# One block pair of a retention and softplus feed-forward kernel moved from plain products to the seven-product scheme

## The chip, the cores and the metric

The kernel runs on one core of a Trainium2 chip. The metric is the device time of one execution in microseconds (us), the median over repeated runs. Engines are named as in the profile: PE is TensorE, PEld its weight loads, DVE is VectorE, ACT is ScalarE, POOL is GpSimd, SP is SyncE, whose queue issues nearly all DMAs (SPq).

## The reference

Eight sequences of 576 positions, eight heads of 64, go through a retention: scores with a decay that depends on the distance, masked to earlier positions, times the values. The 4608 x 512 result is multiplied by w_in (512 x 2048), passed through a softplus and multiplied by w_out (2048 x 512).

```python
ret = scores * Dmat[None, :, :, :]        # scores = q k^T / 8, Dmat = gamma_h ** (i - j) for i >= j, else 0
attn = np.matmul(ret, v)
x = attn.transpose(0, 2, 1, 3).reshape(B * S, H * D)
h = x @ w_in
g = np.maximum(h, 0.0) + np.log1p(np.exp(-np.abs(h)))
return (g @ w_out).astype(np.float32)
```

## The kernel before, in words

All matrix products of the feed-forward part are float32-accurate products of split numbers: every operand is kept as a head and a rest, and one product of a 256 x 128 block of weights with 512 tokens is six matmuls of 128 x 128 x 512 (three terms, two row tiles; `product`, L1094). Tokens are dealt in units of 512, NUNIT = 9 of them. The attention part runs in chunks of 128 tokens: a *group* (`chunk_products`) does the scores and state sums of one chunk and the values of the chunk before it, in some hundred small matmuls, and is put between the large products of the feed-forward part. It writes the PSUM banks `two` and `third`, and for some chunks also `acc`. After the group DVE empties these banks (`scores_out`, `halves_out`, `states_out`), and SP loads the keys and the values of the next group (`next_steps`: `load_keys`, `load_rest`); POOL scales the values (`scale_values`, L229) before the next group's matmuls may read them. For most groups PE also waits, before the second half of its state sums, for a one-column ACT copy (`marker`, L419).

Unit 0 is done in the opening. Units 1 and 2 are the *first pass*, the part that changes. Their hidden layer is cut into NJ = 8 pairs of column blocks. A pair can be done in two ways:

- *Plain*: two slots (`plain_slot`) in unit 1 and two in unit 2. A slot has two products into one bank (`product(bank, xa, True)`, `product(bank, xb)`), ACT's softplus, the head and rest of the result, the outputs of the slot before (`output_some(CPU)`, 12 matmuls, L597 with L605 for unit 0) and, in some slots, a group.
- *Seven-product* (`strassen_pair`): seven products cover both units at once. The products need combined inputs (blocks T1, T2, T3, NT4, made by `start_combined` from four 128 x 256 operations and `finish_combined` from one ACT copy and one DVE subtraction for each of four columns of 128 tokens) and combined weights (`prepare`: load a pair, `prepare_whole`, `prepare_sums`, `prepare_split`, `prepare_store`). The results of unit 2 are kept in DRAM (`kept_dram`) and fetched after unit 2's plain slots, in the *kept loop* (`kept_parts`).

With PLAIN = 4 the order is: 8 slots of unit 1 (pairs 0 to 3), four seven-product pairs (4 to 7), 8 slots of unit 2, the kept loop. Then come three passes that use seven products throughout (`full_pair`, `full_phase`), which the change doesn't touch but which need all combined weights (`sums_dram`), the split second weights (`wout_dram`, written by `raw_store`) and their combined form (`outs_dram`, by `whole_out`, `combine_out`, `split_out`, `store_out`).

The order of each engine's instructions is the order in the program, written out by hand: `schedule(...)` lists which helper runs in which slot, and `jobs`, `blocks`, `starts` and `before` are its places in a slot. Weight blocks come through a ring of 7 tiles: each `product` takes one and issues the load of the block seven products on (`block_load`, L759). The SP queue runs in order, so a DMA that waits holds up those behind it.

In the seven-product pair the bank `acc` takes four products in turn, and is read between them:

```python
product(acc, T3)
nc.vector.tensor_add(c[1], acc, c[1])
...
output_some(2 if few else -(-len(outputs) // 2))
product(acc, NT4)
```

`few` is true when only one slot's four outputs are pending, which is so in the first such pair alone.

## Time and profile before

| what | value |
| --- | --- |
| median of 3 runs | 811.35 us (810.53 to 812.31) |
| profiled execution | 811.05 us, span 809.1 us |
| PE busy | 802.9 us, 99% of the span |
| DVE, ACT, POOL busy | 573.5, 395.7, 135.9 us |
| granted TensorE clock | 1.00 throughout |

The span is what the profile's rows cover; the profiled execution's own time is 1.95 us longer than its span. All times of rows are us from the start of the span. In the rows, a line such as "acc<-xt,ring" names the tile written and the tiles read.

### The profile page before, as it was taken

The page shows a single profiled execution, that of the slowest core. Times are in us where ns is not written, and L with a number is a line of the kernel's source. Part 1 is how long each engine was busy: PE and PEld are TensorE (multiplying, and loading weights), DVE is VectorE, ACT ScalarE, POOL GpSimd, SP SyncE. Part 2 cuts the span into 40 slices and gives each one's busy share as a digit, 9 for nine tenths or more (in the row PEclk, how much of TensorE's full clock was granted, in tenths as well). Part 3 has the DMA queues.
Part 4 walks back from the last instruction along what each step waited for, and adds up shares of the span by engine and source line. Part 5 has one row for each costly group of instructions (what it writes and reads, how often), then busy time and mean ns, then how long its engine had stood idle before and what let it go on. Part 6 is the DMA issues. An engine that isn't in the chain of part 4 may idle for free.

```text
span 809.1 us, 18743 instructions
## 1 busy us (share of the span) xinstructions
PE 802.9 (99%) x7363; PEld 660.7 (82%) x7363; DVE 573.5 (71%) x946; ACT 395.7 (49%) x691; POOL 135.9 (17%) x211
## 2 busy tenths in 40 slices
PE   8999999999999999999999999999999999999998
PEld 6788888888888888888888888888888888888886
DVE  6988878866657973888579974546679944335785
ACT  6877773344333443454345654343355734435553
POOL 4331333611113420121121001111100000000000
PEclk9999999999999999999999999999999999999999
DMA  9999698898987984799987778778767776666665
GB/s 357 366 310 383 233 355 292 303 347 270 311 300 258 383 317 169 255 325 332 298 268 235 216 242 252 240 245 257 214 182 219 220 245 192 193 194 194 205 209 172
DMA packets 150488, 213.59 MB, mean 264 GB/s; under 512 B 10881, under 2 KB 114817, under 8 KB 150401
## 3 DMA queue, kind: packets, MB, share of 16 engines
q1 hardware_dynamic: 150304, 212.40, 78.8%
q8 instruction: 59, 0.97, 0.5%
q14 instruction: 29, 0.23, 0.1%
q10 hardware_dynamic: 96, 0.00, 0.0%
HBM read 169.36 MB, written 42.99 MB: 262 GB/s over the span
## 4 chain that ended last, share of the span: by engine, by line
PE 97%; DMA 2%; ACT 0%; DVE 0%; issue 0%; SPq 0%; DVEq 0%
PE acc L1094 22%; PE sum L1399 21%; PE third L1094 11%; PE y L597 11%; PE h L558 6%; PE y L605 5%; PE two L1094 5%; PE two L1399 4%; PE third L1399 2%; PE acc L1399 2%; PE third L253 2%; PE two L236 2%; PE two L325 1%; PE two L337 1%; DMA raw<-whole 1%; DMA part<-first 0%
## 5 line engine op out<-in xcount | busy, mean ns | idle before, releaser
L1094 PE MATMUL acc<-xt,ring 128*128 128x512 f32 x780 | 196.6, 389 | 0.0
L1399 PE MATMUL sum<-parts,ring 128*128 128x512 f32 (+1 forms) x723 | 173.8, 391 | 0.0
L1094 PEld LDWEIGHTS acc<-xt,ring 128*128 128x128 f32 x780 | 146.3, 188 | 30.6
L1399 PEld LDWEIGHTS sum<-parts,ring 128*128 128x128 f32 x723 | 134.2, 188 | 28.3
L1393 DVE TENSOR_TENSOR parts<-g,parts 128x512 fp32r<-128x512 f32 x168 | 113.5, 692 | 45.8 <-ACT parts L1389 44.6
L1389 ACT CAST parts<-g 128x512 fp32r<-128x512 f32 x168 | 103.7, 622 | 68.0 <-PE sum L1399 24.8
L1094 PE MATMUL third<-xt,ring 128*128 128x512 f32 x408 | 102.8, 389 | 0.0
L581 ACT ACTIVATE g<-g 128x512 f32<-128x512 f32 x96 | 59.0, 631 | 76.5 <-DVE g L1421 35.7
L597 PE MATMUL y<-wout,g 128*128 128x512 f32 x384 | 93.7, 393 | 0.2 <-issue 0.2
L1094 PEld LDWEIGHTS third<-xt,ring 128*128 128x128 f32 x408 | 76.5, 188 | 16.2 <-DVE xt L549 0.4
L597 PEld LDWEIGHTS y<-wout,g 128*128 128x128 f32 x384 | 71.1, 188 | 15.8 <-issue 0.6
L229 POOL TENSOR_TENSOR qv<-qv,consts_sb 128x256 f32<-128x256 f32 x61 | 48.8, 802 | 157.7 <-DMA qv<-others 147.4
L1421 DVE TENSOR_TENSOR g<-two,g 128x512 f32<-128x512 f32 x24 | 16.6, 692 | 52.8 <-PE two L1094 52.8
L558 PE MATMUL h<-xt,win 128*128 128x512 f32 x192 | 47.4, 395 | 0.0
L1419 ACT COPY g<-acc 128x512 f32<-128x512 f32 x24 | 14.1, 587 | 68.1 <-PE acc L1094 68.1
L605 PE MATMUL y<-wout,g 128*128 128x512 f32 x192 | 46.3, 390 | 0.0
L1094 PE MATMUL two<-xt,ring 128*128 128x512 f32 x180 | 45.6, 390 | 0.0
L605 PEld LDWEIGHTS y<-wout,g 128*128 128x128 f32 x192 | 35.9, 188 | 7.6
L558 PEld LDWEIGHTS h<-xt,win 128*128 128x128 f32 x192 | 35.3, 188 | 7.9 <-POOL xt L508 0.2
L590 DVE TENSOR_TENSOR g<-ab,g 128x512 fp32r<-128x512 f32 x40 | 30.5, 762 | 14.2 <-ACT g L586 14.0
L586 ACT CAST g<-ab 128x512 fp32r<-128x512 f32 x40 | 24.7, 617 | 31.1 <-PE y L597 30.3
L1094 PEld LDWEIGHTS two<-xt,ring 128*128 128x128 f32 x180 | 33.7, 188 | 7.2 <-DVE xs L523 0.3
(204 smaller groups left out, 1246.0 us busy)
## 6 DMA issues: line engine op xcount, KB each, us to landing
ring<-split SPq DMA_DIRECT2D x116, 256.0 KB, 4.5
ring<-combined SPq DMA_DIRECT2D x112, 256.0 KB, 3.9
ring<-outcombined SPq DMA_DIRECT2D x96, 256.0 KB, 3.4
qv<-others SPq DMA_DIRECT2D x61, 320.0 KB, 5.0
ring<-outsplit SPq DMA_DIRECT2D x72, 256.0 KB, 3.6
keys<-others SPq DMA_DIRECT2D x61, 256.0 KB, 5.1
wst<-w SPq DMA_DIRECT2D x12, 1024.0 KB, 9.2
split<-win SPq DMA_DIRECT2D x16, 512.0 KB, 9.3
```

Of the source, the lines that this page charges most:

```text
L229: nc.gpsimd.tensor_mul(v, v, f.unsqueeze(2).broadcast_to([P, 4, D]))
L558: nc.tensor.matmul(h, wins[p][:, a, kt * P:(kt + 1) * P], xt[:, b, T1 + kt // 2, kt % 2], start=(n == 0), stop=(n == 3 * NKT - 1))
L581: nc.scalar.activation(out, h, AF.Softplus)
L586: nc.scalar.copy(g[:, HI], ab)
L590: nc.vector.tensor_sub(g[:, LO], ab, g[:, HI].bitcast(F32))
L597: nc.tensor.matmul(ys[u][tt], g[:, a, tt * P:(tt + 1) * P], wouts[p][:, b], start=(p == 0 and n == 0), stop=(p == NF - 1 and n == 2))
L605: nc.tensor.matmul(ys[u][tt], gs[u, p][:, a, tt * P:(tt + 1) * P], wouts[p][:, b], start=p == 0 and n == 0, stop=p == NF - 1 and n == 2, s ...
L1094: nc.tensor.matmul(bank, w[:, ta, kt * P:(kt + 1) * P], xt[:, tb, x, kt], start=start and k == 0, stop=k == 5, skip_group_check=True)
L1389: nc.scalar.copy(t[:, HI], g_slot(J, n))
L1393: nc.vector.tensor_sub(t[:, LO], g_slot(J, n), t[:, HI].bitcast(F32))
L1399: nc.tensor.matmul(bank[m][:, at], w[:, a, m * P:(m + 1) * P], t[:, b, at], start=start and n == 0, stop=n == 2, skip_group_check=True)
L1421: nc.vector.tensor_add(c11, y, c11)
```

## The change

PLAIN becomes 3: pairs 0 to 2 are plain (6 slots in each unit) and pairs 3 to 7 are done by seven products. In unit 1 the four groups go to slots 0, 2, 3 and 5 (before: 0, 2, 4, 6), and slot 3, like slot 0, runs its outputs ahead of its group and uses the bank `third`. The combined weights of pair 4 are formed ahead of slot 3's products, those of pairs 5, 6 and 7 inside the seven-product pairs. The helpers that make the combined inputs of the 512 tokens are moved forward, the last column into slot 5. The first seven-product pair runs three of its four pending outputs after its second product. The combined second weights of pair 0 and five of the eight raw stores move to the kept loop.

```diff
-PLAIN = 4
+PLAIN = 3
+BEHIND = 0, 3
+FIRST_GROUPS = 0, 2, 3, 5
...
-        opens = u == 1 and p == 0
-        bank = two[:, 0] if u == 2 and p == 0 else acc if p % 2 == u - 1 or (u, p) == (1, 1) else later["third"]
+        opens = u == 1 and p in BEHIND
+        bank = acc if (p != 3 if u == 1 else p % 2 or p == 0) else later["third"]
...
+    def raw_now(j):
+        raw_store(j)
+        queued_some(len(queued))
...
+    blocks = schedule((3, prepare_sums, PLAIN + 1))
     jobs = schedule(
         (0, prepare_whole, PLAIN),
-        (1, prepare, PLAIN + 1), (1, prepare_sums, PLAIN), (1, half_b22, 0), (1, whole_out, 0),
-        (2, prepare_split, PLAIN), (2, prepare_whole, PLAIN + 1),
-        (3, prepare_store, PLAIN), (3, finish_combined, 0, nc.vector), (3, half_b22, 1), (3, prepare_sums, PLAIN + 1),
-        (4, prepare_split, PLAIN + 1),
-        (5, prepare_store, PLAIN + 1), (5, finish_combined, 1, nc.vector), (5, half_b22, 2), (5, combine_out, 0),
-        (6, prepare, PLAIN + 2), (6, split_out, 0),
-        (7, store_out, 0), (7, finish_combined, 2, nc.vector), (7, half_b22, 3), (7, finish_combined, 3, nc.vector),
-        *[(3 + 2 * j, raw_store, j) for j in range(3)])
-    starts = schedule((3, start_combined, 1), (5, start_combined, 2), (6, start_combined, 3, nc.vector))
-    soon = schedule((0, start_combined, 0))
+        (1, prepare, PLAIN + 1), (1, prepare_sums, PLAIN), (1, half_b22, 0), (1, prepare_split, PLAIN),
+        (2, prepare_store, PLAIN), (2, prepare_whole, PLAIN + 1), (2, finish_combined, 0, nc.vector),
+        (3, half_b22, 1), (3, prepare_split, PLAIN + 1),
+        (4, prepare_store, PLAIN + 1), (4, finish_combined, 1, nc.vector), (4, start_combined, 2, nc.vector),
+        (4, half_b22, 2), (4, prepare, PLAIN + 2), (4, finish_combined, 2, nc.vector), (4, raw_store, 0),
+        (5, finish_combined, 3, nc.vector), (5, half_b22, 3))
+    starts = schedule((2, start_combined, 1))
+    soon = schedule((0, start_combined, 0), (5, start_combined, 3, nc.vector))
     for p in range(2 * PLAIN):
-        group = groups.pop() if p % 2 == 0 else None
-        plain_slot(1, p, B11, B21, rest, group, (), *(x.get(p, ()) for x in (jobs, starts, soon)))
+        group = groups.pop() if p in FIRST_GROUPS else None
+        plain_slot(1, p, B11, B21, rest, group, blocks.get(p, ()), *(x.get(p, ()) for x in (jobs, starts, soon)))
...
-        output_some(0 if few else -(-len(outputs) // 4))
+        output_some((3 if J == PLAIN and not s else 0) if few else -(-len(outputs) // 4))
...
-    extras, late_sums = {NJ - 2: 1, NJ - 1: 2}, {PLAIN: PLAIN + 2, PLAIN + 1: PLAIN + 3}
+    extras, late_sums = {NJ - 2: 1, NJ - 1: 2}, {J: J + 2 for J in range(PLAIN, NJ - 2)}
...
-                (4, prepare_ring, 2, 2, 4), (5, prepare_ring, 3, 0, 2), (6, prepare_ring, 3, 2, 4),
-                *[(2 * j, prepare_sums, j) for j in range(4)], *[(2 * j + 1, prepare_split, j) for j in range(3)],
-                *[(2 * j + 2, prepare_store, j) for j in range(3)],
-                (2, whole_out, 3), (3, combine_out, 3), (5, split_out, 3), (6, store_out, 3),
-                (4, finish_combined, 0, nc.vector), (6, finish_combined, 1, nc.vector),
-                *[(2 * j - 7, raw_store, j) for j in range(4, NJ)], (4, raw_store, 3))
-            starts = schedule(*[(1 + 2 * i, start_combined, i) for i in range(CPU)])
+                (4, prepare_ring, 2, 2, 4),
+                *[(2 * j, prepare_sums, j) for j in range(3)], *[(2 * j + 1, prepare_split, j) for j in range(3)],
+                *[(2 * j + 2, prepare_store, j) for j in range(2)],
+                (3, whole_out, 3), (5, combine_out, 3),
+                (2, finish_combined, 0, nc.vector), (4, finish_combined, 1, nc.vector),
+                *[(2 * j - 1, raw_store, j) for j in (1, 2)])
+            starts = schedule((0, start_combined, 0), *[(2 * i - 1, start_combined, i) for i in range(1, CPU)])
...
-                                 ((0, 1), finish_combined, 2, nc.vector),
-                                 ((1, 0), half_x, B11, STAGE[0, 0], whole, nc.vector),
-                                 ((1, 1), finish_combined, 3, nc.vector),
+                                 ((0, 1), split_out, 3), ((0, 1), prepare_store, first - 1),
+                                 ((1, 0), half_x, B11, STAGE[0, 0], whole, nc.vector), ((1, 0), store_out, 3),
+                                 ((1, 1), finish_combined, 2, nc.vector),
                                  ((2, 0), half_x, B22, STAGE[1, 1], whole, nc.vector),
-                                 ((2, 1), prepare_split, first - 1), ((2, 1), prepare_store, first - 1)):
+                                 ((2, 1), finish_combined, 3, nc.vector),
+                                 ((3, 0), whole_out, 0), ((3, 1), combine_out, 0),
+                                 ((4, 0), split_out, 0), ((4, 1), store_out, 0),
+                                 *[((n, 1), raw_now, 3 + n) for n in range(5)]):
```

## Rows read from the trace of the kernel before

**Rows 1.** The page: busy time by engine; the chain's share by engine.

```profile
PE 802.9 (99%) x7363; PEld 660.7 (82%) x7363; DVE 573.5 (71%) x946; ACT 395.7 (49%) x691; POOL 135.9 (17%) x211
...
PE 97%; DMA 2%; ACT 0%; DVE 0%; issue 0%; SPq 0%; DVEq 0%
```

**Rows 2.** Windows by stage: length, busy PE, PEld, DVE, ACT, POOL, clock, DMA share, GB/s.

```profile
116.35:168.70 52.35, 52.35 (x689) 43.38 (x689) 40.57 (x64) 19.91 (x38) 22.37 (x29) 1.00 0.88 311
168.70:235.20 66.50, 66.31 (x733) 54.06 (x733) 40.93 (x71) 28.58 (x49) 9.88 (x18) 1.00 0.87 296
235.20:284.50 49.30, 49.30 (x661) 40.81 (x661) 42.09 (x77) 17.25 (x31) 20.41 (x27) 1.00 0.91 325
284.50:309.20 24.70, 24.70 (x109) 20.37 (x110) 17.47 (x22) 10.77 (x15) 5.56 (x8) 1.00 0.74 281
```

**Rows 3.** The chain in order of time, unit 1's slots: start, length, work.

```profile
119.07 2.72 PE y L605 x12
123.81 2.95 PE acc L1094 x12
...
134.05 2.94 PE y L597 x12
...
160.31 2.95 PE y L597 x12
```

**Rows 4.** The chain, first seven-product pair: the product of T1, outputs.

```profile
171.42 1.61 PE third L1094 x6
...
177.80 1.36 PE y L597 x6
```

**Rows 5.** DVE's timeline, slot 1: first and last of four operations of `prepare_sums`.

```profile
128.88 0.96 DVE L798 TENSOR_TENSOR quad<-quad 128x256 f32<-128x256 f32 x1
...
131.39 0.83 DVE L801 TENSOR_TENSOR quad<-quad 128x256 f32<-128x256 f32 x1
```

**Rows 6.** ACT's timeline: softplus and two head copies of slot 2; a `finish_combined` copy.

```profile
132.24 0.60 ACT L581 ACTIVATE ab<-acc 128x512 f32<-128x512 f32 x1 [3.88 <-PE acc L1094]
...
133.46 1.14 ACT L805 CAST quad<-quad 128x512 fp32r<-128x512 f32 x2
...
167.17 1.05 ACT L548 CAST xt<-quad 128x1024 fp32r<-128x1024 f32 x1
```

**Rows 7.** PE's timeline: first score into `acc`, group 1; second half of sums, group 3.

```profile
132.89 0.27 PE L236 MATMUL acc<-qv,keys 64*64 64x64 f32 x1
...
159.67 0.22 PE L253 MATMUL third<-qv,keys 64*64 64x64 f32 x1
```

**Rows 8.** POOL's timeline: scaling of the values for group 2.

```profile
141.27 0.92 POOL L229 TENSOR_TENSOR qv<-qv,consts_sb 128x256 f32<-128x256 f32 x1 [4.96 <-DMA qv<-others]
142.68 1.07 POOL L229 TENSOR_TENSOR qv<-qv,consts_sb 128x256 f32<-128x256 f32 x1 [0.49 <-DMA qv<-others]
```

**Rows 9.** SP queue's timeline: first and last of four loads issued after group 1.

```profile
133.89 0.34 SPq L173 DMA_DIRECT2D keys<-others  x1
...
136.06 0.33 SPq L179 DMA_DIRECT2D qv<-others  x1
```

**Rows 10.** Windows, slots 2 and 3.

```profile
129.48:142.43 12.95, 12.95 (x162) 10.72 (x161) 10.88 (x20) 4.79 (x9) 4.79 (x8) 1.00 1.02 374
```

**Rows 11.** DVE's timeline, first seven-product pair: the addition that reads `acc`.

```profile
177.84 0.69 DVE L1268 TENSOR_TENSOR quad<-acc,quad 128x512 f32<-128x512 f32 x1 [1.29 <-PE acc L1094]
```

**Rows 12.** DVE's timeline after group 3: rest of the softplus, combined inputs.

```profile
162.51 0.68 DVE L590 TENSOR_TENSOR g<-ab,g 128x512 fp32r<-128x512 f32 x1
...
164.31 0.42 DVE L541 TENSOR_TENSOR quad<-xs 128x256 f32<-128x256 f32 x1
...
165.44 0.42 DVE L544 TENSOR_TENSOR quad<-xs,quad 128x256 f32<-128x256 f32 x1
...
168.25 1.23 DVE L549 TENSOR_TENSOR xt<-quad,xt 128x1024 fp32r<-128x1024 f32 x1 [0.26 <-ACT xt L548]
```

**Rows 13.** SP queue's waits, 116 to 310: line, cause, total, times, longest.

```profile
SPq L759 <- DMA combined<-quad: 10.2, 2, 5.2
```

## The prediction

> **What bounds the kernel now.** I read the page first: PE is busy for 99% of the span and makes up 97% of the chain that ended last [rows 1]. DVE, at 71%, and ACT, at 49%, run beside it. The windows by stage say the same of the place that changes: in unit 1's slots, in unit 2's slots and in the kept loop PE is busy for the whole stretch, and in the seven-product pairs for all but 0.19 us [rows 2]. So in these 192.85 us no other engine sets the time. A gain can only come from fewer matmuls, and a loss only from a wait that isn't there today. The chain in order of time gives the price of PE's work: twelve matmuls of 128x512 take 2.72 us, so one takes 0.2267; right after a group of small matmuls twelve take 2.94 or 2.95, which is 0.22 for the restart [rows 3]. A group takes about 2.02 us (from 119.07 + 2.72 = 121.79 to 123.81). Where the cover is thin is read from the timelines of the other engines; those rows come with their terms below.
>
> **The matmuls saved.** A plain pair has two products in each of two slots in each of two units, 8 products of 6 matmuls, 48. A seven-product pair has 42. Outputs and groups stay in number (12 groups up to the kept loop in both). Six matmuls at 0.2267 are **-1.36 us**. The seven-product pair adds four ACT copies and three DVE additions to its surroundings; those stages have DVE at 62% (40.93 of 66.50) [rows 2], so I cost them at nothing as work. Only where PE waits for one of them do they count.
>
> **Pair 3's combined inputs.** Today the first seven-product pair loses 0.25 us: T1's product takes 1.61 us where six matmuls take 1.36 [rows 4], because DVE is late with T1. In the new order the last column is only begun after the group in slot 5. After that group DVE needs 2.88 us until the rest of the softplus is done (160.31 to 162.51 + 0.68), four operations 1.55 (164.31 to 165.44 + 0.42), ACT's copy 1.05 [rows 6] and the subtraction 1.23 [rows 12], together about 6.8 with the handovers. PE meanwhile has 12 outputs (2.95), two products (2.72) and the three outputs put ahead (nine matmuls, 2.04): 7.71. T1 is ready about 0.9 us early, so the old wait goes: **-0.25**. The cover fails if POOL runs beside those four operations, which then take 3.3 us as in slot 1 (128.88 to 131.39 + 0.83) [rows 5]; that would be 0.9 late. I expect POOL idle then, since it waits for loads; ends 0.25 gained, 0.65 lost.
>
> **Slots 1 to 3.** Two new waits, which overlap. First: `prepare_split` for pair 3 is now in slot 1, behind `prepare_sums` in the same slot. The sums end at 132.22 [rows 5], as POOL slows them. ACT then makes two head copies, 1.14 us [rows 6], ahead of slot 2's softplus in its own order. Today the softplus starts at 132.24 and ends at 132.84, and the first score of group 1 into `acc`, the bank that the softplus reads, starts at 132.89 [rows 6, 7]: there is no slack. With the copies ahead, the softplus ends at about 133.9, and PE stands in the middle of group 1 for about 1.05. Second: group 2 moves from slot 4 to slot 3. Without a wait it would start at 134.05 + 2.94 + 2.72 + 2.72 = 142.43 [rows 3]. Its state sums read values that POOL has scaled only at 142.68 + 1.07 = 143.75 [rows 8]; the second half of them is wanted some 0.2 after the start. Alone that is 1.1. With PE already 1.05 late it adds 0.1, if the loads land when they do now. They are issued after group 1 (the keys wait for its sums), so 1.05 later; if all of this reaches the landing, both waits count in full, 2.2. The DMA engines are saturated in these slots, 374 GB/s at a share of 1.02 [rows 10], so the loads stand in a line that a later issue hardly changes. I take **+1.2**; ends 1.1 and 2.2.
>
> The Trainium skill ("DMA: Bandwidth & Descriptors", section on the anatomy of one DMA) would fit a transfer as about 2.0 us plus its bytes at 436 GB/s, which for a load of 320 KB is an estimated 2.75 us. By that rule the second wait would not exist and the term would be 1.05. The trace disagrees: the last of these loads is issued at 136.06 [rows 9] and its scaling begins, released by its landing, at 142.68 [rows 8], 6.6 us later.
>
> **Slot 5, group 3.** It follows group 2 by 2.95 + 2.72 + 2.72 = 8.39 us, where two slots with a group each were 13.1 apart. Two things can be late. The scaled values: for group 2 it took 9.86 us today from the first load's issue (133.89) to the end of the scaling (143.75) [rows 8, 9]; in the new order fewer transfers stand ahead (no raw store, no second store), and I reckon 8 to 8.5. And the `marker` copy on ACT: slot 4 now has both `finish_combined` 1 and the whole of column 2 on DVE and ACT, so that DVE's clearing of the banks (2.2 [rows 3, 12]), a subtraction for the column (0.4), the split (1.2), a rest (0.6), 1.23, 1.55 and then ACT's 1.05, its softplus 0.60 and the marker 0.2 make 9.0 to 10. PE wants the marker for the second half of the sums, which starts 0.64 before a group's end (159.67 against 160.31 [rows 3, 7]), that is 8.39 + 2.02 - 0.64 = 9.8 after group 2. I take **+0.4** for both; ends 0 and 2.3, the latter in the rival below.
>
> **Pair 3, T3 to NT4.** The four pending outputs are now spent: three after the second product, one after B22. Today six of their matmuls, 1.36 us [rows 4], stand between T3's product and NT4's, and hide DVE's addition that reads `acc`, which starts 0.04 after T3 and takes 0.69 [rows 11]. Now nothing does. PE waits 0.73 and pays a restart like the 0.22 after a group: **+0.95**; ends 0.73 and 1.0. Nothing else in this pair gets short: the bank `two` is wanted a full product after the group, as `acc` goes first.
>
> **What I cost at nothing.** Unit 2's slots: DVE is at 85% (42.09 of 49.30 [rows 2]) and loses two slots' rests, one group, a ring sum and a split with the two slots, so its share doesn't rise. One more weight pair loaded, one more kept result stored and fetched, and one ring block less are 1.75 MB, some 5 us of transfers spread over the first pass; the moved raw stores fall into the kept loop, where the DMA share is 0.74 and DVE is at 17.47 of 24.70 [rows 2]. If that cover is gone, a kept result comes late at the price of the delay; ends 0 and 0.5.
>
> **The sum.** -1.36 - 0.25 + 1.2 + 0.4 + 0.95 = +0.94. On the profiled execution's 811.05 us that gives 812.0; the median, 811.35, is 0.3 above it, so I forecast 812.2 for the median. About 0.2%, 1.6 us, is what a measurement of this kernel can tell from no change; this lies inside.
>
> **Rivals.** *The waits don't come*: the handmade order hides the head copies, the loads and the addition. Then -1.36 - 0.25 = -1.61, 809.7. This is also the most that the change can give. For it: PE has no wait today in any slot. Against: each of the three is in the order of an engine that runs in order, with no slack in rows 7, 8 and 11. *Late loads decide, slower*: in slot 3 SP comes to the ring load of pair 3's first combined block, which must wait for the store issued in slot 2; group 2's loads stand behind it. Such waits of SP exist today, two with 10.2 us in all [rows 13], with nothing urgent behind them. If SP is free one us after group 2's sums and the loads then take 9.86 as before, group 3 waits 0.9 + 9.86 - 8.39 = 2.4 in place of 0.4; without that hold 1.5. That gives +2.0 to +2.9, 813.3 to 814.3. It decides from about 9.2 us between group 2's end and the end of the scaling. Against: less is queued ahead than in the rows. *The change saves no time at all because the added stage work is on the path*: 0.0 plus the waits partly, near 811.4; DVE's 62% speaks against it.
>
> **How the numbers follow.** Forecast 0.52 (its own range 811.6 to 812.9, nearly all within 0.2%); waits don't come 0.15 (half of it over 0.2% faster, half within); late loads 0.28 (slower); no gain at all 0.05 (within). Faster: 0.08; within: 0.50 + 0.07 + 0.05 = 0.62, of which 0.02 I give to faster for terms that I overrate; slower 0.28 and 0.02 from the forecast's upper edge. The range 810.0 to 814.2 leaves out the low end of the second case and the top of the third.
>
> **What would show it.** In the new profile: 7,357 matmul records before losses; PE idle or its small matmuls stretched by about a microsecond in group 1 with the softplus after two head copies; group 2's sums released by POOL's scaling; about 0.7 us between T3 and NT4 of the first seven-product pair, released by DVE; T1 of that pair at 1.36. The prediction is wrong if group 1 still ends 1.85 us after its slot's product (132.2 to 134.05 today [rows 3, 6]), if the loads for group 2 land earlier than today, or if unit 2's slots or the kept loop, which I leave alone, show waits.

## The result, and the profile after

The changed kernel takes 815.0 us in the median of 5 runs (813.84 to 817.02) against 811.35 (810.53 to 812.31): a ratio of 1.0051, 95% interval 1.0039 to 1.0062. It is slower, by about 3.7 us, where I had forecast 812.2 and a range up to 814.2. The profiled execution took 815.75 us (span 814.0) against 811.05.

The page of the changed kernel, busy time by engine and the chain's share:

```profile
PE 803.2 (99%) x7357; PEld 660.5 (81%) x7357; DVE 572.9 (70%) x951; ACT 397.7 (49%) x695; POOL 128.1 (16%) x207
...
PE 90%; DMA 4%; DVE 3%; ACT 1%; issue 0%; POOL 0%; SPq 0%; ACTq 0%; DVEq 0%; POOLq 0%
```

The six matmuls are gone (7,357 for 7,363), PE is still "99% busy", and yet its share of the chain fell from 97% [rows 1] to 90%. That is the first sign: the chain now leaves PE for DMA, DVE and ACT. The windows by stage say where (columns as in [rows 2]: unit 1's slots and the first pair's first products, the rest of the pairs and unit 2's first slots, unit 2's last slots, the kept loop):

```profile
116.37:160.00 43.63, 42.78 (x645) 35.18 (x644) 33.12 (x56) 15.77 (x30) 16.66 (x24) 1.00 0.87 300
160.00:250.00 90.00, 87.78 (x930) 71.77 (x929) 54.84 (x100) 37.14 (x64) 11.96 (x23) 1.00 0.86 292
250.00:285.00 35.00, 34.10 (x490) 28.14 (x489) 30.34 (x50) 11.53 (x21) 18.29 (x24) 1.00 0.86 294
285.00:314.19 29.19, 28.12 (x124) 22.99 (x123) 22.77 (x32) 14.10 (x21) 5.71 (x6) 1.00 0.94 348
```

PE idles 0.85, 2.22, 0.90 and 1.07 us in these four stretches, 5.0 in all; before it was 0.19 in the whole first pass [rows 2]. A pause costs more than its idle time, since the matmuls behind it start slowly: below, the six of NT4's product take 1.66 and 1.65 us behind a wait, and 1.36 without one. Everything behind the first pass is unchanged: it takes 495.8 us in either kernel from the first product of the next pass to the last matmul. The pass itself grew from 192.86 to 197.81 us. The view of PE's waits from 110 to 320 us (line, cause, total, times, longest) names the larger ones:

```profile
PE acc L1096 <- DVE quad L1273: 2.2, 2, 1.4
PE y L599 <- DVE g L592: 1.1, 1, 1.1
PE third L255 <- POOL qv L231: 0.9, 1, 0.9
PE acc L238 <- ACT right_edge L421: 0.8, 1, 0.8
```

Before, the same stretch has none of them. The chain in order of time shows each (start, length, work; lines of the kernel have moved down by two to five): group 1; T3 to NT4 of the first seven-product pair; NT4 of pair 5; unit 2's last group; the first kept result.

```profile
131.49 0.76 DVE quad L803
132.28 1.14 ACT quad L807 x2
133.41 0.49 ACT ab L583
133.97 0.26 PE acc L238
...
170.39 0.70 DVE quad L1273
171.13 1.66 PE acc L1096 x6
...
194.26 0.45 SPq L770
194.75 7.32 DMA quad<-split
202.10 0.70 DVE quad L775
...
205.10 0.61 DVE quad L1273
205.75 1.65 PE acc L1096 x6
...
273.05 6.97 DMA qv<-others
280.14 0.62 POOL qv L231
280.81 0.27 PE third L255
...
287.05 2.29 DVE quad L811 x2
289.34 0.89 DVE quad L800
...
291.48 0.61 DVE g L592
292.13 0.96 PE y L599 x3
```

The reader is to see in each of the five stretches which engine hands over to PE and what it did just before. The first is the sequence that the prediction described: the sums end, ACT makes two head copies, only then the softplus that frees `acc`. The second too: DVE's addition lies bare between two products. The third and the fourth begin with a DMA, 7.32 and 6.97 us from its issue to its end. The fifth is DVE's own order: two subtractions of a weight split (L811) and the four operations of `combine_out` (L800 to L803) stand ahead of the rest of the first kept result (L592).

Set against before, place by place, from the two chains, each wait with the slow start behind it:

| place | forecast | measured |
| --- | --- | --- |
| six matmuls; T1 on time; a pause of 0.49 in before's pair 7 | -1.61 | -2.10 |
| group 1 (2.88 from product's end to outputs; 1.85 before) | +1.05 | +1.03 |
| group 2 (2.19; 2.02 before) | +0.15 | +0.17 |
| group 3 (2.39; 2.03 before) | +0.4 | +0.36 |
| pair 3, T3 to NT4, and the start of pair 4 | +0.95 | +1.08 and +0.25 |
| pair 5, NT4 | 0 | +1.71 |
| unit 2, last group | 0 | +1.12 |
| kept loop, first result | 0 | +1.34 |
| sum (the pass: +4.95) | +0.94 | +4.96 |

### The profile page after: what moved, and what is told of

It is laid out like the page before. It is cut to its first block, busy times and chain, and to the rows that moved or that the text cites. A ratio compares the mean times of both kernels' runs of the same rounds, so it can differ in the third digit from the quotient of the medians.

```text
span 814.0 us, 18752 instructions
## 1 busy us (share of the span) xinstructions
PE 803.2 (99%) x7357; PEld 660.5 (81%) x7357; DVE 572.9 (70%) x951; ACT 397.7 (49%) x695; POOL 128.1 (16%) x207
## 4 chain that ended last, share of the span: by engine, by line
PE 90%; DMA 4%; DVE 3%; ACT 1%; issue 0%; POOL 0%; SPq 0%; ACTq 0%; DVEq 0%; POOLq 0%
PE acc L1096 21%; PE sum L1407 20%; PE third L1096 10%; PE y L599 8%; PE h L560 6%; PE y L607 5%; PE two L1096 5%; PE two L1407 4%; PE third L1407 2%; PE acc L1407 2%; PE third L255 2%; PE two L238 1%; PE two L327 1%; PE two L339 1%; DMA raw<-whole 1%; DMA quad<-split 1%
## 5 line engine op out<-in xcount | busy, mean ns | idle before, releaser
L1096 PE MATMUL acc<-xt,ring 128*128 128x512 f32 x804 | 203.2, 390 | 2.2 <-DVE quad L1273 2.2
L1096 PEld LDWEIGHTS acc<-xt,ring 128*128 128x128 f32 x804 | 150.6, 188 | 34.5 <-DVE quad L1273 3.1
L1096 PE MATMUL third<-xt,ring 128*128 128x512 f32 x384 | 96.9, 389 | 0.0
L1096 PEld LDWEIGHTS third<-xt,ring 128*128 128x128 f32 x384 | 72.1, 188 | 15.0
L231 POOL TENSOR_TENSOR qv<-qv,consts_sb 128x256 f32<-128x256 f32 x61 | 43.6, 716 | 175.6 <-DMA qv<-others 170.1
L592 DVE TENSOR_TENSOR g<-ab,g 128x512 fp32r<-128x512 f32 x38 | 29.2, 768 | 9.9 <-ACT g L588 9.8
L323 POOL TENSOR_TENSOR s<-s,consts_sb 128x256 f32<-128x256 f32 (+1 forms) x31 | 25.1, 811 | 69.7 <-DVE s L321 59.5
```

Of the source, the lines that this page charges most:

```text
L231: nc.gpsimd.tensor_mul(v, v, f.unsqueeze(2).broadcast_to([P, 4, D]))
L323: nc.gpsimd.tensor_mul(s, s, f.unsqueeze(2).broadcast_to([P, 2 * n, D]))
L592: nc.vector.tensor_sub(g[:, LO], ab, g[:, HI].bitcast(F32))
L1096: nc.tensor.matmul(bank, w[:, ta, kt * P:(kt + 1) * P], xt[:, tb, x, kt], start=start and k == 0, stop=k == 5, skip_group_check=True)
```

## The experiments

The theory after the result: the waits that I had named are what they are (group 1 and group 2 overlap), and the rest, about 4.2 us in the profile, comes from three places that I had left alone, because the shorter passes bring work and transfers closer to those who need them. Rivals: the named waits don't overlap and count singly; the added bytes make the loads late everywhere; each wait taken away comes back elsewhere. All ratios are against the kernel before on the same chip; "the pass" is the profiled time from the first product of unit 1's slots to the first product of the pass behind.

**1. Pair 3's split a slot later.**

```diff
-        (1, prepare, PLAIN + 1), (1, prepare_sums, PLAIN), (1, half_b22, 0), (1, prepare_split, PLAIN),
-        (2, prepare_store, PLAIN), ...
+        (1, prepare, PLAIN + 1), (1, prepare_sums, PLAIN), (1, half_b22, 0),
+        (2, prepare_split, PLAIN), (2, prepare_store, PLAIN), ...
```

> The changed kernel with pair 3's head copies moved from slot 1 back to slot 2, behind that slot's softplus. Theory of order, with the two waits of slots 1 to 3 overlapping: the 1.07 us in group 1 goes (it ends 1.85 us after its product), group 2 then waits about 1.1 us for POOL's scaling in place of 0.17, and the time falls by 0.2 us at most against 815.0. Rival, independent waits: group 2 keeps its 0.17 us and the whole 1.07 us is won. Rival, volume of transfers: PE waits stay in sum, since the transfers are the same.

Measured: 815.31 us (813.66 to 818.67), ratio 1.0057 [1.0035, 1.008]. Group 1's wait is gone, and group 2 waits for POOL. The waits, and the chain into group 2:

```profile
PE third L255 <- POOL qv L231: 1.2, 1, 1.2
```

```profile
136.84 6.50 DMA qv<-others
143.47 1.00 POOL qv L231
```

From slot 2's first product to the end of group 3 it takes 27.07 us, 26.98 in the changed kernel: nothing is won. So the two waits lie one over the other, as the prediction had them, and the rival of single waits falls. The profiled execution is the slowest of the five (818.67 us): it also holds a pause of 2.42 us in pair 6's group that no engine releases, of a kind that comes up again in runs 2 and 9.

The load took 6.50 us until it landed. By the Trainium skill ("DMA: Bandwidth & Descriptors", section "Anatomy of one DMA") 320 KB would take an estimated 2.75 us. That section gives its fit for DMAs issued on GpSimd; these loads are issued by SP, here and where the prediction used it, and the trace's 6.50 shows that it doesn't carry over to them.

**2. Pair 3's four outputs two and two** (two behind the second product and two behind T3, none behind B22).

```diff
-        output_some((3 if J == PLAIN and not s else 0) if few else -(-len(outputs) // 4))
+        output_some((2 if J == PLAIN and not s else 0) if few else -(-len(outputs) // 4))
...
-        output_some(1 if few else -(-len(outputs) // 3))
+        output_some((0 if J == PLAIN and not s else 1) if few else -(-len(outputs) // 3))
```

> The changed kernel with the four pending outputs of the first seven-product pair dealt two after the second product, none after B22 and two between T3 and NT4, where the change has three, one and none. Theory of order: the wait of NT4's product for DVE's addition goes, T3 to the end of NT4 falls from 2.44 us by 1.08 us apart from the six outputs now between, T1 is still ready or at most 0.2 us late, and the time falls by about 0.9 us. Rival, volume: no change of the time.

Measured: 816.8 us (812.92 to 821.74), 1.0074 [1.0037, 1.0111]. In the profile (813.94, pass 195.85) the wait of pair 3 is gone, so its place and size were right. The time didn't follow: two pauses of PE, 0.8 and 0.6 us, in which it waits for nothing that the profile shows, and a wide spread. Such pauses are the subject of runs 9 to 14.

**3. Pair 7's sums behind the addition** (the sums that pair 5 makes for pair 7 go behind the addition that NT4 waits for).

```diff
-        if more is not None:
+        if more is not None and more < NJ - 1:
...
+        if more == NJ - 1:
+            prepare_whole(more)
+            prepare_sums(more)
```

> The changed kernel with DVE's sums of the last weight pair (pair 7, in the third seven-product pair) moved behind the addition that NT4 waits for. Theory of order: the loads land as late as before, about 202 us, but hold up only themselves; the wait of 1.4 us and its restart of 0.3 us before NT4 go, and the time falls by 1.3 to 1.7 us. Rival, volume: the wait comes back at another place, for instance at the bank emptied after the group, and under 0.5 us is won.

Measured: 814.67 us (813.24 to 816.49), 1.0054 [1.0034, 1.0075]; pass 194.91. Pair 5 doesn't wait; pair 3's 0.8, the kept loop's 1.3 and 0.4 of group 1 remain. One profile doesn't show that it was the edit: in runs 2 and 5 pair 5 doesn't wait either, without it. Over all profiles, four of the six with the old order wait there (0.3 to 1.4 us), and none of the eight with this edit. Run 9 is the closest comparison: its weights land as late after the pair's first product as those of run 4 (9.13 and 9.18 us), and only run 4, without the edit, waits, for 0.46.

**4. Slot 3's second ring load behind the group's loads** (units 1 and 2).

```diff
-        product(bank, xb)
+        behind_group = p == 3
+        product(bank, xb, load=not behind_group)
...
+        if behind_group:
+            block_load()
```

> The changed kernel with one ring load, that of slot 3's second product in either unit, issued behind the loads of that slot's group in place of ahead of them. Theory of order: SP no longer stands at a store's landing in front of the group's loads, these are issued about 2 us earlier in unit 2's slot 3, the values for the last group there are scaled before it starts, its 0.9 us wait goes, and the time falls by 0.8 to 1.0 us. Rival, volume: the loads land at the same time as before whatever SP's order, since the DMA engines are the limit, and the 0.9 us stays.

Measured: 813.92 us (813.28 to 815.33), 1.004 [1.0025, 1.0055]; pass 195.74. SP's queue in the changed kernel, its wait over 110 to 320 us and then its timeline:

```profile
SPq L761 <- DMA combined<-quad: 22.5, 5, 6.4
```

```profile
264.45 0.86 SPq L819 DMA_DIRECT2D combined<-quad  x2
...
269.76 0.52 SPq L761 DMA_DIRECT2D ring<-combined  x1
...
271.02 0.96 SPq L175 DMA_DIRECT2D keys<-others  x1
```

and the timeline with the load put behind:

```profile
262.88 0.86 SPq L819 DMA_DIRECT2D combined<-quad  x2
...
267.36 0.91 SPq L175 DMA_DIRECT2D keys<-others  x1
...
271.09 1.92 SPq L761 DMA_DIRECT2D ring<-combined  x2
```

SP stands at the ring load until the store issued 5.3 us before has landed, here for 1.3 us (before, 10.2 us in two such waits [rows 13]; the corresponding store in unit 2 lay 16.7 us ahead, issued at 254.50 for a load at 271.22). The group's loads are behind it. With the edit the keys are issued 4.5 us after the store in place of 6.6, and the scaling ends 2.27 us before the last group's first matmul in place of 1.30 behind it. The last group doesn't wait then. In the eight profiles with the edit the scaling ends 1.1 to 2.3 us before the group. In the other five with the old order it lies between 1.02 before it and 0.81 behind, and only run 5's waits, for 0.4: this wait sits at the edge and comes in some executions. Before, the scaling ended 0.51 ahead.

**5. The changed kernel again**, no edit.

> The changed kernel once more, unaltered, beside the runs of this call, for its spread. Theory of order: 814 to 816 us with the fixed waits of group 1 (1.0 us), of NT4 in the first seven-product pair (1.0) and of the kept loop (1.1 to 1.5) in every profile; the waits on loads (pair 7's weights, the values of unit 2's last group) come and go between executions. Theory of chance alone: the fixed waits differ too.

Measured: 816.23 us (814.29 to 820.14), 1.0078 [1.0062, 1.0095]. In this profile (814.29, pass 195.73) group 1 waits 0.8, pair 3 0.8 and the kept loop 1.1 again, the last group 0.4, and pair 5 not at all. So three waits are there again; those that hang on a landing come and go.

**6. The kernel before with eight more stores of 256 KB** in its seven-product pairs (more bytes than the change adds; the copies are read by nobody).

```diff
+    again_dram = [dram.tile([P, 2, T], F32, name=f"again{j}") for j in range(NJ)]
...
+        nc.sync.dma_start(again_dram[J][:, 0], ab2)
...
+        queued.append(lambda: nc.sync.dma_start(again_dram[J][:, 1], ab3))
```

> The kernel before, with every kept half result stored twice (a second copy to a DRAM tile that nothing reads): 8 more transfers of 256 KB, 2.1 MB, where the change adds 1.75 MB. Theory of order: PE still waits nowhere in unit 1's and unit 2's slots, and the time rises by 0 to 0.7 us. Rival, volume of transfers: the loads of the groups and of the weights land later, PE waits for them, and the time rises by 2 to 4 us, as with the change.

Measured: 810.79 us (810.41 to 811.6), 0.9999 [0.9991, 1.0008]. The rival of the bytes falls: 2 MB more cost nothing where they hold up no queue. These stores lie in the seven-product pairs; that transfers just ahead of an urgent load can delay it is another matter, and run 10 bears on it.

**7. The edits of 2, 3 and 4 together**, and `combine_out` 3 from unit 2's last slot into the kept loop.

```diff
-                (3, whole_out, 3), (5, combine_out, 3),
+                (3, whole_out, 3),
...
+                                 ((0, 0), combine_out, 3), ...
```

> The changed kernel with four edits together: outputs two and two in the first seven-product pair, the sums of pair 7 behind the addition that NT4 waits for, slot 3's ring load behind its group's loads, and the combination of pair 3's second weights (its DVE additions) moved from unit 2's slot 5 to the kept loop. Theory of order: the waits of NT4 (1.0), of pair 7's weights (up to 1.7), of unit 2's last group (up to 1.0) and of the kept loop (1.1 to 1.5) go, the ones of slots 1 to 5 (about 1.6) stay; the time is 811 to 812 us, about that of the kernel before. Rival, volume: the loads stay late, and the time stays over 813.5.

Measured: 812.03 us (811.31 to 815.52), 1.0026 [1.0014, 1.0039]; pass 194.57. PE's waits that are left:

```profile
PE acc L1096 <- issue: 0.9, 1, 0.9
PE acc L238 <- ACT right_edge L421: 0.8, 1, 0.8
PE y L599 <- DVE g L592: 0.7, 1, 0.7
```

Half to two thirds of the loss is back, by the ratios (1.0026 for 1.0051 and 1.0078). The kept result still waits 0.7, since the two subtractions of pair 2's split stand ahead of it.

**8. The head copies and group 1's loads moved as well** (pair 3's split to slot 2, pair 4's load behind group 1's loads, pair 4's sums in slot 3 and its split in slot 5).

```diff
-    blocks = schedule((3, prepare_sums, PLAIN + 1))
+    blocks = {}
...
+        (2, prepare, PLAIN + 1), (2, prepare_split, PLAIN), (2, prepare_store, PLAIN), ...
+        (3, half_b22, 1), (3, prepare_whole, PLAIN + 1), (3, prepare_sums, PLAIN + 1),
...
+        (5, finish_combined, 3, nc.vector), (5, half_b22, 3), (5, prepare_split, PLAIN + 1),
```

> As the run before, and in unit 1 also pair 3's head copies in slot 2 behind its softplus, the load of pair 4's weights behind the loads of group 1 instead of ahead of them, and pair 4's sums in slot 3, its split in slot 5. Theory of order: group 1 doesn't wait, group 2's values are scaled some 2 us earlier, since 1 MB fewer stands in the line ahead of their loads, so that its wait falls from 1.1 us to under 0.2; the time is 810 to 811 us, up to 1.4 us below the kernel before, which is the six matmuls. Rival: moving these steps puts a wait elsewhere in slots 3 to 5, and the time is that of the run before or more.

Measured: 814.87 us (813.12 to 819.58), 1.0062 [1.004, 1.0085]; pass 196.4. A miss. Groups 1 and 2 don't wait, but the wait came back at group 3:

```profile
PE third L255 <- ACT right_edge L421: 1.5, 1, 1.5
PE two L339 <- issue: 1.3, 1, 1.3
```

DVE's sums for pair 4, put into slot 3, delay the last steps of column 2, and so ACT's copy and the marker behind it. The rival of waits that move was right here.

**9. Pair 2's split and store into the kept loop**, on the kernel of 7.

```diff
-                ..., *[(2 * j + 1, prepare_split, j) for j in range(3)],
+                ..., *[(2 * j + 1, prepare_split, j) for j in range(2)],
...
+                                 ((1, 1), prepare_split, first - 1), ((1, 1), prepare_store, first - 1),
```

> The four edits of the run before last (outputs two and two, the late pair's sums behind the addition, the ring load behind the group's loads, combine_out 3 moved into the kept loop) with one more: the split and the store of pair 2's combined weights go from unit 2's last slot into the kept loop, a part that comes after the first kept result. My theory (the first kept result waits in DVE's order behind the two subtractions of the split, 2.4 us, and what stood behind them): the wait of the first kept output, 0.7 us there, goes, and the profile's waits keep only group 1's (0.8); median about 811.3. Rival (the kept result itself lands late, whatever DVE does before): the wait stays at 0.6 to 0.7, median 812.0. Second rival: the split now delays a later kept result, and the wait comes back one place on, 812.

Measured: 812.72 us (810.61 to 816.09), 1.002 [1.0007, 1.0034]. The kept loop's 132 outputs now run without a gap (30.17 us), as my theory said; the median is not what it said. Five of the twelve runs lie at 810.6 to 811.2, the others at 812.0 to 816.1. The profile is one of the latter (815.49, pass 196.81). Its chain in pair 6's group, and the windows behind it (columns as in [rows 2]):

```profile
224.25 2.75 issue
...
227.33 2.38 PE y L599 x6
229.71 2.17 PE acc L1096 x6
```

```profile
224.25:227.00 2.75, 0.00 (x1) 0.00 (x1) 0.00 (x0) 0.17 (x1) 0.00 (x0) 1.00 0.91 258
227.00:229.70 2.70, 2.70 (x11) 2.15 (x12) 2.28 (x5) 0.00 (x0) 0.00 (x0) 0.66 0.92 304
229.70:232.00 2.30, 2.30 (x9) 1.78 (x8) 1.80 (x3) 0.70 (x2) 0.92 (x1) 0.66 0.20 69
232.00:234.00 2.00, 2.00 (x10) 1.65 (x9) 0.64 (x2) 1.45 (x2) 0.00 (x0) 1.00 0.26 88
```

PE stood for 2.75 us with nothing to wait for, and afterwards the granted clock was 0.66 in the mean of 5.0 us. From 227.87 to 231.28 us it was at 0.50, the lower of the two levels (1.2 GHz): twelve matmuls took 4.55 us, where after a group they take 2.94 to 2.95 [rows 3]. In run 1's profile the pause of 2.42 us is followed by the lower level too, from 228.32 to 231.73.

**10. Unit 0's stores held back through slots 0 to 2**, and pair 3's split in slot 2, on the kernel of 9.

```diff
+        if not hold:
             queued_some(1 + (len(queued) > 7))
...
-        product(bank, xa, True)
+        behind_group, early = p == 3, u == 1 and p < 3
+        product(bank, xa, True, hold=early)
```

> The same and two edits more: pair 3's split goes from slot 1 to slot 2 (as in the first experiment), and the queued stores of unit 0's outputs, some 1 MB, are held back through slots 0 to 2 of unit 1. My theory (the loads for group 2 are late because they stand behind other transfers): group 1's wait goes, and group 2's, which was 1.2 us with the split moved alone, falls to 0.3 or less; group 3 follows group 2; about 1 us less than the run above, 810.3, below the kernel before. Rival (POOL's own order decides when the scaling starts, or the time of a load does not hang on what is queued): group 2 waits for POOL by about 1.2 us again, and the time is that of the run above, 811.3. Second rival: the stores held back collide with later loads, and slot 5 or the seven-product pairs show new waits of DMA.

Measured: 812.05 us (811.13 to 815.31), 1.0021 [1.001, 1.0032]; pass 192.21. The loads' half was right: groups 1 and 2 don't wait (POOL's scaling ends at 143.4, when group 2 is still to begin; in run 1, with the split moved alone, group 2 waited 1.2 for it). The last of the loads lands 5.6 us after its issue here, 6.5 in run 1: the stores queued ahead did delay it, by about 0.9. What is left is one wait, at group 3 again:

```profile
PE third L255 <- ACT right_edge L421: 1.1, 1, 1.1
```

**11. Pair 4's split and store in slot 5**, on the kernel of 10.

```diff
-        (3, half_b22, 1), (3, prepare_split, PLAIN + 1),
-        (4, prepare_store, PLAIN + 1), ...
+        (3, half_b22, 1),
...
+        (5, prepare_split, PLAIN + 1), (5, prepare_store, PLAIN + 1))
```

> The run with the stores held back, and one edit more: the split and the store of pair 4's combined weights go from slots 3 and 4 to slot 5, behind the last column. My theory (in that run the marker of group 3 was late by 1.1 us because DVE had 1.6 us of this split ahead of the column's four operations and the ACT copy): group 3's wait goes or falls to 0.3, nothing else appears, and the first pass takes the 2.1 us less than the kernel before that the matmuls saved and two old waits are worth. In the time: about 1.1 less than that run, 810.9 in the median, and 809.8 where the opening is not late. Rival (the scaled values of group 3 are just as late): a wait of 0.5 to 1 for POOL takes the marker's place, median 811.7. Second rival: the pauses of issue at matmuls 2246 and 2622 stay in some executions, so single runs of 812 to 815 remain whatever the waits do.

Measured: 811.22 us (808.78 to 814.95), 1.0009 [0.9994, 1.0023]. No wait for another engine is left in the view of PE's waits; its profile has one pause of issue, 1.3 us. The quickest runs, 808.78 and 809.55, lie below all of the kernel before (809.81 to 814.84 there), the slowest at 815: the second rival, that the pauses stay, is right too.

**12. The code moved by 40 matmuls**: 20 of 25 rounds of fill matmuls left out at the start (their results are read by nobody), on the kernel of 11.

```diff
-FILLS = 25
+FILLS = 5
```

> The same, with 20 of the 25 rounds of tiny fill matmuls of the opening left out (they compute nothing that is used), 40 matmul records fewer ahead of everything. In all profiles of the changed kernel with a pause of issue, it lies at the same matmul, the 2246th or the 2622nd, at the end of a group, and a 16 KB instruction load lands 1.0 to 1.5 us before it ends. If these are fixed places in PE's code where the next piece must have been loaded, leaving out 40 records moves them 40 matmuls on, out of the group into the large products, where PE needs 9 us for 40 matmuls: no pause at these places, and the single runs of 812 to 815 go; spread about 1 us as in the kernel before, median 810.5. Rival (the pauses come from the traffic at that time, not from the place in the code): pauses at the same places in the work, 190 to 193 and 224 to 227 us, and the same spread. Second rival: the places move into another group, and pauses show there.

Measured: 811.72 us (811.01 to 814.9), 1.0017 [1.0005, 1.0029]. In the profile the first pass has no wait and no pause (191.19 us). But what comes behind it takes 3.0 us longer, with pauses at 496.19 (0.76) and 567.47 us (1.58): the second rival. The pauses hang on the place in the code, and in this place they fall into another group.

**13 and 14. The code moved by 8 matmuls**, four more rounds of fill: on the changed kernel as it is, and on the kernel of 11.

```diff
-FILLS = 25
+FILLS = 29
```

> The changed kernel as it is, with four more rounds of the opening's tiny fill matmuls (eight matmul records, 16 instructions with their weight loads, some 0.15 us; nothing uses what they compute). The instruction loads of all profiles stand in a row: 59 loads of 16 KB, one for each 256 instructions of PE, and every pause of issue lies at such a boundary, where the load began less than 2.8 us before PE came to it. The piece that ends at matmul 2622 is passed in 2.6 us in the changed kernel, since it is little more than one group; 16 instructions on it takes 4.3 us, as 1.4 us of large products come into it. If the passing time is what makes the load late: fewer pauses, the single runs lie closer together (813.5 to 815.5 rather than up to 820) and the median falls by about 1 us to 814.5; the unpriced waits stay, so it remains slower than the kernel before. Rival (the pauses have nothing to do with the places of the pieces): the same spread and median as the changed kernel's, 815 to 816.

> The last but one run's kernel (every wait named so far taken away, pair 4's split in slot 5) with the same eight records more. It has no wait of PE left in the first pass; its profile had one pause of issue, 1.3 us at matmul 2246. If the passing time of the pieces counts: most runs 809.0 to 810.3, median 809.9, below the kernel before by 0.1%. Rival (same spread whatever the places): median 811.2 again, single runs up to 815.

Measured: the changed kernel 814.17 us (813.45 to 814.8, 5 runs), 1.0039 [1.0027, 1.0052], pass 196.8; its waits are there (0.8 us in group 1, 0.8 in pair 3, 1.2 in pair 5, 1.5 in the kept loop), its spread is gone, as far as five runs tell (813.84 to 820.14 over the eleven runs without the move). The kernel of 11: 809.78 us (809.1 to 810.98, 11 runs), 0.9987 [0.9978, 0.9996], faster than both kernels, by 0.13% than the kernel before. The kernel before was not run with its code moved. The whole first pass as one window, changed kernel first, then this one:

```profile
116.37:314.19 197.82, 192.79 (x2184) 158.08 (x2183) 141.07 (x236) 78.54 (x136) 52.61 (x77) 1.00 0.87 302
```

```profile
116.61:307.97 191.36, 191.28 (x2183) 157.82 (x2183) 141.83 (x236) 78.77 (x136) 56.01 (x77) 1.00 0.89 313
```

PE is busy for 191.28 of 191.36 us. The pass is 1.50 shorter than the 192.86 of before. That is more than the six matmuls' 1.36, but the 192.86 hold the pause of 0.49 and T1's 0.25, which are not in every execution: run 6's profile, of the order of before with the copies added, has neither and takes 192.09. Against that, 0.73 is won: 1.36 less 0.40 in group 3 and some 0.2 at the start of pair 4. The chain of run 14 still comes to group 3's second half from ACT's marker (154.74 to 154.80, the first matmul at 154.84), and the group takes 2.43 us in place of 2.03; the busy share hides it, since PE idles only 0.08 there.

## Why the prediction was wrong

**Right: what the change saves.** "-1.36" for six matmuls and "-0.25" for T1. T1's product takes 1.36 us in the new profile; it does so in run 6's too, so that the 0.25, read from one profile of before, need not be a saving in every execution. The six matmuls' share follows from the count (7,357) and the sum of the table; the most that any run won in the median is 1.2 us (run 14, 809.78 against 810.98), with group 3 still late.

**Right: slots 1 to 5 and pair 3.** The waits that I priced, group 1's softplus behind the head copies, group 2's scaling, group 3's marker and NT4's bare addition, come to 2.64 us in the table against 2.55 forecast (2.89 with pair 4's start), each released by the engine that I had named. Run 1 shows that groups 1 and 2 overlap, run 2 that NT4's wait goes with two outputs between. Pair 4's start is a small miss: "Nothing else in this pair gets short" left out the bank `two` behind the group.

**Wrong: "What I cost at nothing"** (0, ends 0 and 0.5). In the profile this step is worth 4.17 us: 1.71 in pair 5, 1.12 in unit 2's last group, 1.34 in the kept loop. In two more profiles of the same work (runs 5 and 13) the same three places come to 2.3 and 3.3. Unit 2's slots and the kept loop are what the prediction had named at its end as a case that would make it wrong; pair 5 it had counted only as bytes ("One more weight pair loaded"). I had argued from shares: DVE at 85% in unit 2's slots and at 17.47 of 24.70 in the kept loop, a DMA share of 0.74. Shares said nothing on order. Three places stood behind it. For the kept loop an edit shows the cause plainly; for the other two, where the wait comes only in some executions, the edits and the queue's rows together do:

- *The kept loop.* `combine_out` 3 and pair 2's split now stand in unit 2's last slot; DVE comes to the first kept result's rest 0.4 us after PE wants it, and needs 0.6. In every profile that keeps this order PE waits 1.1 to 1.5 us there. Runs 7 and 9 move these two pieces, and the wait falls to 0.7 and then to 0.
- *Unit 2's last group.* The rival "late loads decide" was right in kind and wrong in place: I saw SP stand at a ring load behind a store that has still to land, and priced it in unit 1's slot 3. In unit 1's slot 3 of the changed kernel SP does stand so, for 4.0 us (139.98 to 143.98), and PE doesn't wait for it. In unit 2 the passes of six slots bring the ring load of the next pass's first block up to 5.3 us behind its store; before it was 16.7.
- *Pair 5.* The two loads of pair 7's weights have landed 7.8 us after the first was issued, and the sums made from them stand in DVE's order ahead of the addition that NT4 waits for. With the sums behind the addition nothing waits (runs 3 and 9). The loads are late because they are issued late, and the reason is again SP standing at a ring load:

```profile
181.22 1.48 SPq L819 DMA_DIRECT2D combined<-quad  x2
189.12 3.18 SPq L761 DMA_DIRECT2D ring<-combined  x4
194.26 1.00 SPq L770 DMA_DIRECT2D quad<-split  x2
```

  The store issued at 181.22 has landed at 189.07, and SP stands until then. In the three profiles of this order with the longest waits (1.44, 1.23 and 0.46) the first load is issued 2.3 to 3.4 us after the pair's first product starts, in the other three (0.31 and twice none) 0.5 to 1.2.

Here and in the last group the size is one of chance: other profiles of the same order have 0 to 1.2 and 0 to 0.4.

**Not foreseen at all: pauses of issue.** They add no wait to the profiled execution of the changed kernel; that they add to its other runs is inferred from their times, since those have no rows. With the code moved by 8 matmuls (run 13) the same work has its median at 814.17, without it at 815.0 and 816.23. So of the roughly 3.7 to 5.3 us that the change cost, about 3.2 are waits net of the saving, as run 13 has them, and I put the other 0.5 to 2 down to pauses.

**What the wrong step did to the range.** Its upper end, 814.2, came from the "late loads" rival alone with the other unpriced places at no more than 0.5. With the step at 2.3 to 4.2 in place of 0, the sum of 0.94 becomes 3.2 to 5.1, against a loss of 3.7 to 5.3. Left open is why the stores that SP stands for land earlier in some executions than in others: in pair 4 the first of them has landed 7.85 us after its issue in the changed kernel's profile, 6.69 in run 2's.

## What to carry to other kernels

When stages get shorter, list for each in-order queue and engine what moved closer together: a store and the load that reads it, a load and its user, filler work and the urgent operation behind it; a low busy share doesn't cover any of these. Put work with no deadline behind the operation that the critical engine wants next, and a load that must wait behind the loads that must not. Where a gain doesn't show in the median, look at the spread of single runs before looking for another wait.

## What the runs showed of the hardware

PE's code comes in pieces, and a piece can be late. The page of every run of the changed kernel lists them:

```profile
q8 instruction: 59, 0.97, 0.5%
```

59 loads of 16 KB for 15,136 instructions of PE (each matmul record with its weight load counted as two, each wait of its own as one) is one for 256. Counted so, from the order of the instructions, all the pauses in these profiles that I could place lie at one remainder by 256 (194 or 195): at matmul 2246 or 2622 in the changed kernel and its variants, at 2498 in the kernel before (0.18 us), at 5235 and 6105 in run 12, where 40 records fewer stand ahead. In the traces each load begins 2.2 to 30 us before the first matmul of its piece. In the ten pauses it is 2.2 to 2.7, the low end: PE comes to the end of its piece before that, and stands. Without a pause the shortest is 2.4. Five of the ten:

| profile | load begins | PE stands |
| --- | --- | --- |
| before | 217.92 | 220.17 to 220.35 |
| run 2 | 190.0 | 191.50 to 192.27 |
| run 9 | 224.29 | 224.25 to 227.00 |
| run 11 | 189.9 | 190.86 to 192.18 |
| run 12 | 566.6 | 567.47 to 569.05 |

A piece that is little more than one group is passed quickly: the one that ends at matmul 2622 in 2.9 us in the changed kernel, and in some 4.3 us when the code stands 16 instructions further on, with 1.4 us of large products in it. With that the spread is gone (runs 13 and 14), without any change to the work. It is not the passing time alone, though: a piece passed in 2.2 us in the kernel before had no pause, and those at 2246 take 5.2 to 5.5 us, the pause not counted, and had some. What starts a load early or late is not settled here.
